# Moving a norm's logarithm, exponential and Newton step later in the first attention of a fused attention and feed-forward kernel

## The chip, the cores and the metric

The kernel runs on one core of a Trainium2 chip. The metric is the time of one execution on the device in microseconds (us); three runs of the kernel before the change were timed, and the median is what counts. One more execution was recorded by the hardware profiler.

## The reference

An attention with root-mean-square norms on queries and keys, followed by a feed-forward block with a squared ReLU, all in float32 (the feed-forward weights arrive as 64-bit floats):

```python
batch, n_heads, seq, head_dim = (8, 12, 448, 64)
def rmsnorm(x, g):
    rms = np.sqrt(np.mean(x * x, axis=-1, keepdims=True) + 1e-06)
    return x / rms * g
q_n, k_n = (rmsnorm(q, g_q), rmsnorm(k, g_k))
scores = np.matmul(q_n, k_n.transpose(0, 1, 3, 2)) / np.sqrt(64)
...  # softmax over the keys
attn_out = np.matmul(attn, v)
x = attn_out.transpose(0, 2, 1, 3).reshape(3584, 768)
h = x @ w_in                        # 768 x 2048
out = np.maximum(h, 0.0) ** 2 @ w_out   # 2048 x 768
```

## The kernel before, in words

The feed-forward block works on spans of two batch items (896 tokens); its two products use a seven-product block scheme, so that the weights are first turned into sums and differences of blocks. Heads are handled in pairs: 6 pairs per batch item, 12 pairs for a span. The kernel has these stages, one behind the other:

- a first pair's norm and transposes (`first_pair`);
- the first attention, `attention_alone`, for pairs 0 to 11 of span 0. Nothing but the preparation of the weights runs beside it. It ends at about 133 us, where the first product's matmuls (`pa`, L1091) begin;
- the first product of span 0, in which the rest of the weights is still prepared;
- then, span by span, products with the next span's attention (`attention`, another function) laid between them.

The order of the work is written out by hand: every engine issues its instructions in the order in which the Python code calls them, with semaphore waits put in where an operand needs them. Nothing is reordered by a scheduler. `attention_alone` is a generator with four `yield`s for each pair; at each `yield` the caller runs one or two quarters of a "tick" of the weights (`weights`, `prepare`). A tick rounds 128 rows or columns of a weight to float32. It has L589 and L606 on ScalarE, L603, L608 and L613 on VectorE, the block additions L575 and the sums L583 on GpSimd, loads (L540) and stores (L598) on SP's queue.

Iteration i of `attention_alone` does, between its yields:

1. the load of pair i+3 (L316 queries, L326 keys, on SP's queue); `scores(i, 0)` and `scores(i, 1)`, each of four matmul passes (L804) and two exponentials (L808); the transposes of pair i+1's keys (L779, copied out by L781); the `values` of pair i-1 with key chunks 2 and 3 (L867); `add_up(i, 1)`, a sum of two chunks of exponentials (L821); and `norm(i+2)`: squares on ScalarE (L719), their sums by head (L720), mean and epsilon (L721);
2. the transposes of pair i+1's queries (L779, scaled by L783); the load of values (L701); and `roots(i+2)`, the reciprocal square root of the norm: a logarithm (L730) and an exponential (L731) on ScalarE, one Newton step of three small VectorE instructions (L732 to L734), and on GpSimd the product of the raw queries with it (L735);
3. `scores(i, 2)` and `scores(i, 3)`; `total_of(i-1)`, the softmax sums by matmul (`tot`, L892); the `values` of pair i with chunks 0 and 1; and `finish(i-1)`: a transpose of the sums (L910), a reciprocal (L911), a transpose back (L912) and the product that gives the attention's output (L919), all on VectorE;
4. for odd pairs `add_up(i, 2)` (L821 again); `combine_x(i-1)` (L929 and L932 to L934 on VectorE) for the second batch item.

So `roots(i+2)` is called in iterations 1 to 9, for pairs 3 to 11. What it makes is used in two places: the normalised queries by the transposes L779 of iteration i+1, and the keys' factors as a scale of the exponentials L808 of iteration i+2. Logarithm and exponential share one buffer, `half`; the Newton step also uses `other`; both come from a pool with two buffers.

Of the kernel before, what the change touches and what calls it, by code (L numbers as in the profile page):

```python
# [304 lines left out]
def places_of(qk, i, work):  # L305


    first, second = i % 2 * 4 + work, i % 2 * 4 + 2 + (i // 2 + work) % 2
    return qk[:, first:second + 1:second - first]
# [78 lines left out]
def attention_then_ffn_bounded(  # L388
# [42 lines left out]
    SP = S // NJ  # L431
# [11 lines left out]
    NAT = 2 * NPAIR  # L443
# [21 lines left out]
    qk, qkT, ident, mhalf, gains, rstd0, _ = held  # L465
# [65 lines left out]
    spare, banks = {}, {}  # L531
# [142 lines left out]
    vs, probs, pavs, tots, normed, rstds = {}, {}, {}, {}, {}, {0: rstd0}  # L674
# [3 lines left out]
    def load(i):  # L678
        if i < NAT:
            load_q(nc, qk, q, i)  # L680
            load_k(nc, qk, k, i)
            return

        b, h0 = i // NPAIR, 2 * (i % NPAIR)
        for s, src in enumerate((q, k)):
            dst = by_squares(i, 0)[:, s]
            for n in range(4):
                nc.sync.dma_start(dst[n * 32:(n + 1) * 32],
                                  src[b, h0 + n // 2, :, n % 2 * 32:n % 2 * 32 + 32]
                                  .rearrange("(g t) e -> t g e", t=32))  # L690
# [32 lines left out]
    def roots(i):  # L723


        raw, sq = (places_of(qk, i, n)[:SP] for n in range(2))
        rstd = rstds[i]
        flat = rstd.rearrange("p s n -> p (s n)")
        y, t = (small.tile([P, 2 * S // 32], F32, tag=tag, name=tag)[:SP, 0:4 * NJ] for tag in ("half", "other"))
        nc.scalar.activation(y, flat, AF.Ln, scale=2.0 ** -63)  # L730
        nc.scalar.activation(y, y, AF.Exp, scale=-0.5, bias=sums["rebias"])  # L731
        nc.vector.scalar_tensor_tensor(t, y, -0.5, flat, ALU.mult, ALU.mult)  # L732
        nc.vector.tensor_tensor(t, t, y, ALU.mult)
        nc.vector.scalar_tensor_tensor(flat, t, 1.5, y, ALU.add, ALU.mult)  # L734
        nc.gpsimd.tensor_tensor(sq[:, 0].rearrange("p (j h d) -> p h j d", j=NJ, h=2),  # L735
                                raw[:, 0].rearrange("p (h j d) -> p h j d", j=NJ, h=2),
                                rstd[:, 0].rearrange("p (h j) -> p h j ()", h=2).to_broadcast([SP, 2, NJ, D]),
                                ALU.mult)
# [36 lines left out]
    def transpose(i, s, n):  # L775

        pt = bank("pt", n)
        for j in range(NJ):
            nc.tensor.transpose(pt[:, j * SP:(j + 1) * SP], normed[i][s][:, j * P:(j + 1) * P], ident[:SP, :SP])  # L779
        if s:  # L780
            nc.scalar.copy(qkT[:, i % 2, s], pt)  # L781
        else:
            nc.scalar.activation(qkT[:, i % 2, s], pt, AF.Copy, scale=gains[:, 0:1])  # L783

    def scores(i, c):


        if i >= NAT:
            sc = ps_s.tile([P, 2, 512], F32, tag="s", name="sc")
            n = S if c < NF else S // 2  # L790
            for h in range(2):
                rows = slice(h * D, (h + 1) * D)
                for m, part in enumerate(sides):
                    keys = slice(c * P + m * D, c * P + (m + 1) * D) if c < NF else slice(NF * P, S)
                    of = slice(0, S) if c < NF else slice(m * n, (m + 1) * n)
                    nc.tensor.matmul(sc[part, h, 0:n], qkT[rows, 0, 1, keys], qkT[rows, 0, 0, of], start=True, stop=True)  # L796
            pr = probs[i, c] = places[(NF * i + c) % len(places)] if c < NF else halves[i % 2]
            nc.scalar.activation(pr, sc[:, :, 0:n], AF.Exp)  # L798
            return
        at = i % 2  # L800
        sc = ps_s.tile([SP, 2, 512], F32, tag="s", name="sc")
        for h in range(2):
            rows = slice(h * D, (h + 1) * D)
            nc.tensor.matmul(sc[:, h, 0:S], qkT[rows, at, 1, c * SP:(c + 1) * SP], qkT[rows, at, 0, :],  # L804
                             start=True, stop=True)
        pr = probs[i, c] = places[(NJ * i + c) % len(places)][:SP]
        for h in range(2):
            nc.scalar.activation(pr[:, h], sc[:, h, 0:S], AF.Exp, scale=rstds[i][:, 1, 2 * c + h:2 * c + h + 1])  # L808

    def acc_of(i):  # L810
        return sums[i % 2][:SP] if i < NAT else sums["acc"]

    def add_up(i, c):

        acc = acc_of(i)
        if i >= NAT and c == NF:
            for m, rows in enumerate(sides):
                part = acc[rows, :, m * S // 2:(m + 1) * S // 2]
                nc.vector.tensor_tensor(part, part, probs[i, c][rows], ALU.add)
            return  # L820
        nc.vector.tensor_tensor(acc, probs[i, 0] if c == 1 else acc, probs[i, c], ALU.add)  # L821
# [59 lines left out]
    def added(i):  # L881

        return 3 if i % 2 and i + 1 < NAT else 2

    def total_of(i):


        tots[i] = ps_o.tile([P, S], F32, tag="t", name="tot")
        parts = [acc_of(i)] + [probs[i, c] for c in range(added(i), NJ)]
        for n, pr in enumerate(parts):  # L890
            for h in range(2):
                nc.tensor.matmul(tots[i][h * D:(h + 1) * D, :], sums["ones"], pr[:, h, :],  # L892
                                 start=(n == 0), stop=(n + 1 == len(parts)))
# [6 lines left out]
    def finish(i):  # L900

        b, hp = divmod(i, NPAIR)
        x = factors = xT[:, b % 2, hp]
        if i < NAT:
            pav = pavs.pop(i)


            turned, factors = sums["turned"], sums["factors"]
            few = small.tile([P, S // 32], F32, tag="few", name="few", bufs=1)
            nc.vector.transpose(turned, tots.pop(i))  # L910
            nc.vector.reciprocal(few, turned.rearrange("p (g r) -> p g r", r=32)[:, :, 0])  # L911
            nc.vector.transpose(factors.rearrange("p (g r) -> p g r", r=32),  # L912
                                few.rearrange("p g -> p g ()").to_broadcast([P, S // 32, 32]))

            x = x.rearrange("d (p j) -> d j p", j=NJ)
            pav, factors = (t.rearrange("d (j p) -> d j p", j=NJ) for t in (pav, factors))
        else:
            pav = rests.pop(i)
        nc.vector.tensor_tensor(x, pav, factors, ALU.mult)  # L919
        del vs[i]  # L920
# [15 lines left out]
    def attention_alone():  # L936


        for i in range(NAT):
            more = i + 1 < NAT  # L940
            if 0 < i < NAT - 3:
                load(i + 3)
            scores(i, 0)
            scores(i, 1)
            if i == 0:

                transpose(1, 1, 1)
                scores(0, 2)
                scores(0, 3)
                transpose(1, 0, 0)  # L950
                add_up(0, 1)
                norm(2)
                load_v(1)
                values(0, (0, 1))
                load(3)
                yield
                continue
            if more:
                transpose(i + 1, 1, 0)
            values(i - 1, (2, 3))  # L960
            add_up(i, 1)
            if i + 2 < NAT:
                norm(i + 2)
            elif not more:
                norm(NAT)
                load(NAT + 2)
            yield
            if more:
                transpose(i + 1, 0, 0)
            load_v(i + 1)  # L970
            if i + 2 < NAT:
                roots(i + 2)
            yield
            scores(i, 2)
            scores(i, 3)
            total_of(i - 1)
            values(i, (0, 1))
            finish(i - 1)
            yield
            if added(i) == 3:  # L980
                add_up(i, 2)
            combine_x(i - 1)
            if NAT <= i + 3 < NAT + 2:
                load(i + 3)
            yield
        values(i, (2, 3))
        total_of(i)
        finish(i)
        combine_x(i)
# [639 lines left out]
```

## Time and profile before

| what | us |
|---|---|
| runs | 1347.04, 1347.29, 1348.31; median 1347.29 |
| the profiled execution | 1347.79 |
| its span, first to last instruction | 1346.0 |
| TensorE busy in the span | 1324.7 (98%) |
| VectorE busy | 861.9 (64%) |
| ScalarE busy | 486.4 (36%) |
| GpSimd busy | 681.0 (51%) |
| first attention ends, L1091 begins | 133.1 |
| L730 and L731, 9 times each | 0.22 and 0.31 each |
| L732, L733, L734, 9 times each | 0.17 each |
| L735, 9 times | 1.04 to 1.54 each, median 1.14 |

In the profile PE is TensorE, PEld its weight load, DVE VectorE, ACT ScalarE, POOL GpSimd, SP the queue of SyncE. A line such as L821 is a line of the kernel's file. An instruction is written as what it writes, an arrow to the left, and what it reads, with partitions and elements. The shares of busy time are averages over all stages; the change lies in the first tenth of the span, so that what counts is the view of that stretch. The granted TensorE clock is full speed (0.999 on the mean).

### The profile page before, as it was taken

To read this page: it belongs to the slowest core of one execution; us is meant where nothing else is said; L and a number is where in the kernel's file an instruction comes from. 1 tells how busy PE (TensorE), PEld (TensorE's weight loads), DVE (VectorE), ACT (ScalarE), POOL (GpSimd) and SP (SyncE) were. 2 spreads that over 40 slices of the span, in tenths; PEclk is the share of its full clock that TensorE was granted. 3 is DMA by queue.
4 is the path that set the end of the run, shared out by engine and by line. 5 is a ranking of instruction groups with operands and counts; after the bars stand their busy time and mean duration, and the time that the engine had idled before them with its cause. 6 is when DMAs were issued, how large, how long until landed. Compare 5 with 4: busy or idle time off the path is not lost.

```text
span 1346.0 us, 17761 instructions
## 1 busy us (share of the span) xinstructions
PE 1324.7 (98%) x5930; PEld 698.9 (52%) x5930; DVE 861.9 (64%) x1333; ACT 486.4 (36%) x939; POOL 681.0 (51%) x546
## 2 busy tenths in 40 slices
PE   8999999999999999999999999999999999999997
PEld 3333444444445655444444755444444665556887
DVE  6999788489988233467888533457888823336553
ACT  7886466555541011345553011235554101111000
POOL 5766533466765222647774522447676522322452
PEclk9999999999999999999999999999999999999999
DMA  8977999666665433346755433345664444421333
GB/s 226 244 214 200 312 357 331 187 131 121 138 140 125 104 88 88 102 105 132 149 125 144 110 90 88 92 113 117 134 129 128 107 100 139 131 88 47 115 103 56
DMA packets 413817, 190.18 MB, mean 141 GB/s; under 512 B 282388, under 2 KB 408724, under 8 KB 413716
## 3 DMA queue, kind: packets, MB, share of 16 engines
q1 hardware_dynamic: 406164, 180.21, 51.8%
q0 software_dynamic: 4736, 8.40, 2.5%
q8 instruction: 49, 0.80, 0.3%
q10 hardware_dynamic: 2816, 0.34, 0.2%
q14 instruction: 52, 0.43, 0.1%
HBM read 155.72 MB, written 33.16 MB: 140 GB/s over the span
## 4 chain that ended last, share of the span: by engine, by line
PE 87%; DVE 7%; ACT 4%; issue 1%; DMA 1%; POOL 0%; SPq 0%; DVEq 0%; ACTq 0%
PE ps L1190 21%; PE pd L1091 11%; PE pa L1091 10%; PE pc L1091 10%; PE sc L796 7%; PE pav L878 7%; PE pb L1091 5%; PE ps L1373 3%; PE ps L1241 2%; PE pd L1345 2%; PE pc L1345 2%; PE pa L1345 2%; ACT gT L808 2%; PE pd L1175 1%; PE pc L1175 1%
## 5 line engine op out<-in xcount | busy, mean ns | idle before, releaser
L1067 POOL TENSOR_TENSOR gT<-gT 128x448 f32<-128x448 f32 x96 | 94.2, 983 | 258.0 <-ACT gT L1063 258.0
L761 POOL TENSOR_TENSOR half<-half,mhalf 128x28 f32<-128x28 f32 x36 | 184.1, 5115 | 70.2 <-DVE half L760 56.2
L1190 PE MATMUL ps<-gT,sw 128*128 128x448 f32 x432 | 169.3, 545 | 0.0
L1063 ACT ACTIVATE gT<-gT 128x448 f32<-128x448 f32 x96 | 55.4, 577 | 300.5 <-DVE gT L1106 300.5
L1091 PE MATMUL pa<-xT,sw 128*128 128x448 f32 x384 | 155.0, 540 | 0.6 <-ACT p L1095 0.6
L1190 PEld LDWEIGHTS ps<-gT,sw 128*128 128x128 f32 x432 | 80.1, 190 | 87.2 <-issue 85.2
L1190 PE MATMUL ps<-gC,sw 128*128 128x448 f32 x288 | 113.1, 546 | 0.0
L796 PE MATMUL sc<-qkT 64*64 64x448 f32 (+1 forms) x1152 | 110.1, 497 | 0.3 <-ACT pr L798 0.2
L1091 PEld LDWEIGHTS pa<-xT,sw 128*128 128x128 f32 x384 | 72.7, 190 | 71.8 <-issue 70.5
L583 POOL TENSOR_TENSOR gC<-gC 128x384 f32<-128x384 f32 x64 | 76.4, 1213 | 63.4 <-DVE gC L579 61.7
L1190 PEld LDWEIGHTS ps<-gC,sw 128*128 128x128 f32 x288 | 53.2, 190 | 59.5 <-issue 57.7
L846 POOL DMA_DIRECT2D xT<-factors x72 | 38.1, 534 | 89.9 <-DMA factors<-square 65.2
L1106 DVE TENSOR_TENSOR gT<-z,pd 128x448 f32<-128x448 f32 x32 | 19.8, 620 | 97.8 <-PE pd L1091 97.8
L798 ACT ACTIVATE pr<-sc 128x896 f32<-128x896 f32 x87 | 76.9, 909 | 11.1 <-PE sc L796 11.1
L1091 PE MATMUL pd<-xT,sw 128*128 128x448 f32 x192 | 77.9, 542 | 1.5 <-DVE z L1098 1.4
L763 POOL TENSOR_TENSOR qk<-qk,half 128x448 f32<-128x448 f32 x72 | 76.9, 1089 | 2.8
L1091 PE MATMUL pd<-xC,sw 128*128 128x448 f32 x192 | 77.5, 540 | 0.7 <-DVE gT L1106 0.7
L1091 PE MATMUL pb<-xC,sw 128*128 128x448 f32 x192 | 77.5, 540 | 0.2 <-DVE gT L1106 0.2
L1091 PE MATMUL pc<-xT,sw 128*128 128x448 f32 x192 | 77.5, 540 | 0.0
L1091 PE MATMUL pc<-xC,sw 128*128 128x448 f32 x192 | 77.4, 539 | 0.0
L878 PE MATMUL rest<-pr,vt 64*64 64x448 f32 x348 | 72.7, 537 | 0.0
L878 PE MATMUL pav<-pr,vt 64*64 64x448 f32 x348 | 72.7, 537 | 0.0
(282 smaller groups left out, 2455.1 us busy)
## 6 DMA issues: line engine op xcount, KB each, us to landing
sw<-w1s SPq DMA_DIRECT2D x224, 192.0 KB, 2.4
sw<-w2s SPq DMA_DIRECT2D x102, 256.0 KB, 3.5
w1s<-gC SPq DMA_DIRECT2D x8, 1344.0 KB, 6.9
w2s<-gC SPq DMA_DIRECT2D x8, 1344.0 KB, 6.8
qk<-in_q_dram SPq DMA_DIRECT2D x144, 56.0 KB, 2.6
qk<-in_k_dram SPq DMA_DIRECT2D x144, 56.0 KB, 2.4
xT<-factors POOLq DMA_DIRECT2D x72, 112.0 KB, 3.4
vt<-in_v_dram SPq DMA_DIRECT2D x72, 96.0 KB, 3.8
```

Of the source, the lines that this page charges most:

```text
L583: nc.gpsimd.tensor_tensor(*[blocks_of(n)[:, place_of(n, i)] for i in (dst, x, y)], op)
L761: nc.gpsimd.tensor_tensor(half, half, mhalf, ALU.pow)
L763: nc.gpsimd.tensor_tensor(qkn[:, s], raw[:, s], half[:, s * NG:(s + 1) * NG].rearrange("p g -> p g ()").to_broadcast([P, NG, 32]), ALU.mult)
L796: nc.tensor.matmul(sc[part, h, 0:n], qkT[rows, 0, 1, keys], qkT[rows, 0, 0, of], start=True, stop=True)
L798: nc.scalar.activation(pr, sc[:, :, 0:n], AF.Exp)
L878: nc.tensor.matmul(into, vs[i][rows, h, c, :], probs[i, c][rows, h, :], start=(c == 0), stop=(c == NF), skip_group_check=True)
L1063: nc.scalar.activation(g, src, AF.Relu)
L1067: nc.gpsimd.tensor_tensor(g, g, g, ALU.mult)
L1091: nc.tensor.matmul(ps, stream[n + at][:, c], rhs[:, c], start=first and c == 0, stop=c == HC - 1, skip_group_check=not first)
L1190: nc.tensor.matmul(ps, stream[n][:, c % 4], rhs_of[i][:, c], start=c == 0, stop=c == HF - 1)
L1345: nc.tensor.matmul(ps, lhs[:, c], rhs[:, c], start=first and c == 0, stop=c == HK - 1, skip_group_check=not first)
L1373: nc.tensor.matmul(ps, weights_of(o, m, c // HK)[:, c % HK], rhs_of[i][:, c, part], start=c == 0, stop=c == HF - 1)
```

## The change

`roots` is cut in two. Its logarithm and exponential stay in `roots`, which is called behind `scores(i, 3)` instead of ahead of the yield before it. The Newton step and the product on GpSimd become a function `step`, called behind `finish(i-1)`. The buffers are handed over in a dictionary, `spare`. No instruction is added, removed or altered. The quarters of a weights tick that run at the yield between come ahead of the moved instructions.

```diff
         nc.scalar.activation(y, flat, AF.Ln, scale=2.0 ** -63)
         nc.scalar.activation(y, y, AF.Exp, scale=-0.5, bias=sums["rebias"])
+        spare["root", i] = y, t
+
+    def step(i):
+
+        raw, sq = (places_of(qk, i, n)[:SP] for n in range(2))
+        rstd = rstds[i]
+        flat = rstd.rearrange("p s n -> p (s n)")
+        y, t = spare.pop(("root", i))
         nc.vector.scalar_tensor_tensor(t, y, -0.5, flat, ALU.mult, ALU.mult)
         nc.vector.tensor_tensor(t, t, y, ALU.mult)
         nc.vector.scalar_tensor_tensor(flat, t, 1.5, y, ALU.add, ALU.mult)
...
             load_v(i + 1)
-            if i + 2 < NAT:
-                roots(i + 2)
             yield
             scores(i, 2)
             scores(i, 3)
+            if i + 2 < NAT:
+                roots(i + 2)
             total_of(i - 1)
             values(i, (0, 1))
             finish(i - 1)
+            if i + 2 < NAT:
+                step(i + 2)
             yield
```

On ScalarE L730 and L731 stand behind the four exponentials L808 of scores 2 and 3, and behind the tick's L589 or L606 of that yield. On VectorE L732 to L734 stand behind L919. On GpSimd L735 stands behind the weights' instructions of that yield: it is moved past none to four of L575 and L583.

## The prediction

> **What bounds it.** Over the whole page TensorE is busy 98% of the span, but the change acts only in the first attention, from about 23 us to 114 us, so I read that stretch by itself. The view of stages gives, per 30 us, busy time of PE, PEld, DVE, ACT and POOL:
>
> ```profile
> 30.00:60.00 30.00, 28.07 (x146) 10.94 (x148) 28.36 (x43) 25.59 (x47) 19.11 (x15) 1.00 0.99 241
> 60.00:90.00 30.00, 28.17 (x146) 10.39 (x142) 28.00 (x41) 23.96 (x44) 21.10 (x18) 1.00 0.86 260
> 90.00:120.00 30.00, 28.33 (x148) 10.87 (x148) 29.01 (x40) 24.02 (x43) 21.74 (x16) 1.00 0.64 176
> ```
>
> VectorE (third figure) and TensorE (first) are both at 93 to 97%; ScalarE has 4 to 6 us of slack in each 30. Next, the waits from 20 to 133 us: waiter, what it waited for, us in total, times, longest.
>
> ```profile
> ACT half L730 <- DVE rstd L721: 14.7, 9, 2.6
> ...
> POOL qk L735 <- DVE rstd L734: 12.4, 4, 3.7
> ...
> PE pt L779 <- ACT qkT L781: 3.4, 7, 1.1
> ...
> DVE other L732 <- ACT half L731: 1.4, 6, 0.6
> ...
> DVE gT L821 <- ACT gT L808: 0.9, 1, 0.9
> ```
>
> Almost all of ScalarE's idle time stands before the logarithm L730. VectorE itself waits for another engine only 1.4 + 0.9 us, and 0.2 for a square. So VectorE sets the pace, and how long its own instructions take is the question. From the groups by shape in 24.86 to 117 us (count, busy us, mean ns):
>
> ```profile
> L821 DVE TENSOR_TENSOR gT<-gT 112x896 f32<-112x896 f32 x14 | 22.2, 1595 | 0.9 <-ACT gT L808 0.9
> L608 DVE TENSOR_SCALAR gC<-gC 128x768 uint32<-128x768 uint32 x11 | 11.2, 1014 | 0.1
> ...
> L603 DVE TENSOR_SCALAR gC<-gC 128x768 f32<-128x768 f32 x11 | 7.3, 666 | 0.1
> ```
>
> These means are not the true durations. The timeline has L821 at 1.08 us where GpSimd is idle and at 1.9 us where it is at work; L608 and L603 at 0.55 or 0.9 to 2.8; L613 at 0.95 or 1.3 to 1.7. I call such a lengthened instruction a hit. Between 24.86 and 117 us I count 22, and the excess is 22.2 - 14x1.08 = 7.1 for L821, 11.2 - 11x0.55 = 5.1 for L608, 1.3 for L603, 1.9 for L613, 0.5 for L721: 15.9 us, or 0.72 us a hit. The transposes and products of `finish` (L910 to L919, 2.45 us) and the reduction L720 (1.2 us) are never hit.
>
> **The skill.** The Trainium skill, "SBUF — State Buffer", section "Who interferes with whom", says that a VectorE instruction in a two-port mode, or with two SBUF inputs against a GpSimd instruction that reads SBUF, and GpSimd lock each other out of a shared port pair, whoever is second waiting for the whole instruction; reductions and instructions with one SBUF input outside those modes don't. The trace agrees: 0.82 us more on the two-input L821, none on L720 or L910. "ScalarE: Activation LUTs", section "Table sets: the hidden batching unit", has Ln and Exp in one set; the trace has a single table load, at 0.73 us, so I cost putting Ln between other Exps at nothing.
>
> **The parts.** Nothing is added or removed; 9 norms (pairs 3 to 11) are moved. Call "turn i" the stretch from the Newton step of iteration i to that of i+1.
>
> Ln and Exp (0.22 + 0.31 us, 9 times) go behind the four exponentials L808 of scores 2 and 3. ScalarE's 14.7 us disappear and L808 comes earlier. ScalarE isn't the bound, so this is worth only what others waited for it: the 1.4 us before L732, the 0.9 before L821 and 0.2 before L720, together **-2.5 us** at most. What is late next on ScalarE is L783, which needs the transposed queries.
>
> The Newton step (three instructions, 0.62 us with their gaps) goes behind `finish`. It then finds its exponential long done. But L735, the product on GpSimd that it releases, now starts about 3 us later against VectorE's work. Two rows of the timeline (start us, length us) show the old place, over `finish`, 0.2 us behind the end of Newton at 55.42 (the releaser named, L589, had long ended):
>
> ```profile
> 55.34 0.64 DVE L910 STREAM_TRANSPOSE gT<-tot 128x448 f32<-128x448 f32 x1
> 55.65 1.04 POOL L735 TENSOR_TENSOR qk<-qk,rstd 112x512 f32<-112x512 f32 x1 [2.05 <-ACT gC L589]
> ```
>
> GpSimd's weight work (L575, L583, about 1.0 us each unhit, four or so a turn) queues behind L735 in order. Before, L735 and one or two of those ran under `finish`. After, GpSimd stands waiting for Newton during `finish`, and L735 with its followers runs against L603, L608, L613 and L821. Some weight work is now ahead of L735 and gets the 1.2 us of L720, but that holds one instruction, `finish` two and a half.
>
> I walked the new order of issue for turns 1 to 8: the first VectorE instruction behind Newton goes free (L735 starts 0.2 us after L734), then the engines take the lock in turn, and the instruction right behind an L821 goes free, as in the trace at 71.28. Turn 4 as example. Before: Newton, `finish` (over it L735, L575, L583), L603, L608, L821, L720, L721, L613: the trace has three hits (58.37, 60.50, 63.55). After: Newton, L603 free, L735, L608 hit, L583, L821 hit, L583 and the start of L575 under L720, L613 hit, L575, L603 hit, `finish`: four. By turns, before as seen 1, 3, 3, 3, 3, 1, 3, 2 = 19; after by the walk 3, 4, 3, 4, 3, 4, 5, 2 = 28 (in turn 2 one of the four falls on Newton itself). The same walk over the old order gives 23, so it counts high; the added hits lie between 28 - 23 = 5 and 28 - 19 = 9. I take 7: 7 x 0.72 = **+5.0 us**.
>
> L735 also has a reader, the query transposes L779 of the next iteration. Before, L735 ended 4.0 to 4.7 us ahead of them (46.26 against 50.31). Newton moves by 2.5 to 4.7 us and L735 waits for one VectorE instruction more, so that margin goes; TensorE queues the scores 2 and 3, the totals L892 and the values L867 behind that transpose. While VectorE is behind, that wait is cover, not cost: the loop L910 to L919 2.45, Newton 0.62, wait and L735 1.8, transposes 0.75, scores 1.69, totals 1.65 or 2.48 is about 9.4 us against a turn of 10.4 (83.07 us for 8). At the end of the stage it isn't cover. L779 of pair 11 starts at 113.74, and from there TensorE runs nearly unbroken to 133 us. Newton of iteration 9 follows `finish` at 111.3; add L821 and L929, which go first (1.6), L735 (1.04) and its signals (0.3): 114.2. That is **+0.45 us** besides VectorE's own slip.
>
> Moved past queues: SP's load of a later pair's queries (L316) waits for L735 and delays the keys, values and weight words behind it by some 3 us; but a load issued at 56.72 is squared by L719 at 70.92, so 14 us cover it. If that cover went, L719 would wait. GpSimd issues no DMA here. L575 and L583 ahead of L735 finish some blocks of weights sooner, whose store (L598) waited 21.2 us in all for L583; no engine waited for that store in this stage: nothing.
>
> Sum: -2.5 + 5.0 + 0.45 = **+3.0 us** (2.95), carried to the end, since everything up to 191 us is issued in one fixed order with the weights. The profiled execution took 1347.79 us (span 1346.0 and 1.8 around it), so it would take 1350.8; the runs' median, 1347.29, stands 0.5 below it, so I say 1350.3.
>
> **Unseen, bounded.** The trace shows no turn with L735 behind `finish`. From below: no hit added, only the waits gone, -2.5 + 0.45 = -2.0; the hits may even fall, as VectorE had one of 2.27 us (L608 at 79.45) that needn't recur: -4. From above: 9 hits at a full GpSimd instruction of 1.0 us, +7.0.
>
> **Rivals.** 0.2%, or 2.7 us, is about what a measurement of this kernel can tell from no change.
>
> One, *lock-out decides* (the above): +1.5 with 5 hits, +4.4 with 9; likeliest +3.0; own range 1347.5 to 1352. For it: 19 hits already, and `finish` as the only long shelter. Against: the walk overcounts.
>
> Two, *ScalarE's release decides*, faster: the chain of waits runs through L808 often (12.3% of it in 86 to 120 us), so a freed ScalarE may bring TensorE and VectorE forward. It decides if fewer than 3 hits are added (3 x 0.72 = 2.05), and passes 0.2% if the hits fall by one or more: about -3.2 us, 1344.1.
>
> Three, *TensorE waits for L735*: if L779 is held 0.5 us in each of 8 turns with nothing to cover it, 4 us come on top: +7, 1354.3. Against: the loop of 9.4 us.
>
> Four, *absorbed*: from 163 to 191 us the chain leaves TensorE for the weights' rounding (L589, L603, L608, L579). If the weights' DMA (busy share 1.00 in 150 to 180 us) and not the engines' order sets that, a slip before it vanishes: within 1 us, 1347.3. That the change doesn't do what it says is excluded: the issue orders show the moves in all 9 iterations.
>
> **Chances.** One 0.50, two 0.22, three 0.13, four 0.15. One falls within 0.2% about one time in ten (0.05), four always: same 0.20; slower 0.45 + 0.13 = 0.58; faster 0.22. The range takes in two and three: 1344.0 to 1355.0; beyond either end lies about 0.1.
>
> **What would show it.** Right: L730's wait on L721 gone; L735 starting after L919; hits in 24 to 117 us near 29, L821's mean above 1.7 us; L779 waiting for L735; 'pa' L1091 starting near 136 instead of 133.1. Wrong: mean durations of L821, L608, L613 unchanged or lower, and the first L1091 earlier than 133; or a later start there and the same end, which would be the fourth case.

## The result, and the profile after

The kernel became slower. Median before 1347.28 us (6 runs, 1345.68 to 1348.31), after 1353.55 us (6 runs, 1351.88 to 1355.8): ratio 1.0047, 95% interval 1.0037 to 1.0056. The forecast was 1350.3 us with a range of 1344 to 1355, so the direction is right and the size is 3.3 us short. It lies above the 1347.5 to 1352 us that the prediction gave to the lock-out alone. The profiled execution of after took 1353.08 us, its span 1351.3 us, 5.3 above that of before.

Lines of the changed file carry other numbers: L721 and everything above it keep theirs, L730 and L731 too; L732 to L734 are now L740 to L742; then, before to after, L735 is L743 (the product on GpSimd), L779 L787 (transposes), L783 L791, L804 L812 (scores), L808 L816, L821 L829 (`add_up`), L867 L875, L892 L900 (totals), L910 to L912 L918 to L920, L919 L927, L929 L937, L1091 L1101 (`pa`).

First the view by stages: length, busy time of PE, PEld, DVE, ACT, POOL, then granted clock, DMA share, GB/s.

```profile
30.00:60.00 30.00, 27.32 (x142) 10.79 (x144) 29.23 (x42) 25.46 (x46) 22.16 (x16) 1.00 0.85 236
60.00:90.00 30.00, 28.12 (x148) 10.78 (x144) 29.06 (x40) 24.44 (x45) 22.58 (x15) 1.00 0.75 227
90.00:120.00 30.00, 25.49 (x128) 10.01 (x124) 27.22 (x37) 21.26 (x38) 20.89 (x14) 0.94 0.77 196
```

VectorE is busier than before in the first two stages (29.23 and 29.06 against 28.36 and 28.00) and does fewer instructions there (42 and 40 against 43 and 41). Its instructions got longer. In the third stage something else happens: both TensorE and VectorE fall, and the clock is 0.94.

The groups by shape, VectorE in 24.86 to 121 us (count, busy us, mean ns, idle before):

```profile
L829 DVE TENSOR_TENSOR gT<-gT 112x896 f32<-112x896 f32 x14 | 25.0, 1794 | 0.0
L608 DVE TENSOR_SCALAR gC<-gC 128x768 uint32<-128x768 uint32 x11 | 9.7, 878 | 0.2
...
L603 DVE TENSOR_SCALAR gC<-gC 128x768 f32<-128x768 f32 x10 | 5.5, 550 | 0.0
L721 DVE TENSOR_SCALAR rstd<-rstd 112x16 f32<-112x16 f32 x8 | 5.5, 686 | 0.3
```

The mean of `add_up` goes from 1595 to 1794 ns, 12 of its 14 instructions now being hit. L603 is hit no more (666 to 550), L608 less often (1014 to 878), but the tiny L721, 241 ns on the mean before, now takes 686. Its work is 0.17 us; I read the rest as waiting for the port lock, which the trace shows as busy time.

Then the waits in 20 to 133 us (waiter, what it waited for, us in all, times, longest):

```profile
PEld pt L787 <- POOL qk L743: 14.3, 8, 4.6
...
ACT gT L816 <- PE sc L812: 11.4, 10, 1.7
...
PE pt L787 <- POOL qk L743: 8.2, 5, 3.8
ACT qkT L791 <- PE pt L787: 6.7, 5, 3.3
...
DVE gT L918 <- PE tot L900: 3.3, 3, 2.2
...
ACT half L730 <- DVE rstd L721: 1.9, 2, 1.2
```

ScalarE's wait before the logarithm fell from 14.7 to 1.9 us, and VectorE's waits for ScalarE (1.4 and 0.9) are gone. But the time that ScalarE had stood before the logarithm it now stands before exponentials and query copies, since TensorE is late: TensorE itself waits 8.2 us for the product on GpSimd, a wait that before had no row. And VectorE waits for TensorE's totals.

Last the timeline of TensorE, where that wait is longest (start, length, in brackets the idle time ahead and its releaser):

```profile
105.79 0.92 PE L787 MATMUL pt<-ident,qk 112*128 112x112 f32 x4 [3.84 <-POOL qk L743]
106.64 3.08 PE L812 MATMUL sc<-qkT 64*112 64x448 f32 x8
109.65 2.48 PE L900 MATMUL tot<-gT,ones 112*64 112x448 f32 x12
```

And VectorE's answer to it:

```profile
112.17 0.65 DVE L918 STREAM_TRANSPOSE gT<-tot 128x448 f32<-128x448 f32 x1 [2.15 <-PE tot L900]
```

The four transposes take 0.92 us and the eight scores passes 3.08 behind this gap; elsewhere in this trace, at 118.17 us, they take 0.60 and 1.76. The granted clock of 105 to 110 us is 0.66. The Trainium skill, "TensorE: Matmul & The Clock Gate", section "What's actually happening", has this mechanism: an idle window of some 3.4 us halves the clock. Here a gap of 3.84 us was followed by about 4 us at roughly half speed.

**The balance.** From the Newton step of iteration 1 to that of iteration 9 before took 83.07 us, after 87.54: +4.47. It consists of the waits for ScalarE, -2.5; of the hits, 26 with an excess of 18.4 us against 19 with 13.9, +4.5; and of VectorE's waits for the totals in turns 1 to 8, +2.4 (2.15 of it in the row above). The Newton step stands at another point of VectorE's order than before, so I carry on from an instruction that both kernels have at the same one: the `add_up` behind `finish` of iteration 9 starts at 111.27 us before and 115.14 after, 3.87 later, 0.6 less than the turns say. The end of the stage adds 0.56 to that, and from the last query transposes to `pa` come another 0.85. So `pa` begins at 138.42 instead of 133.14 us, 5.28 later, and the span is 5.3 longer. Nothing was given back.

### The profile page after: what moved, and what is told of

Read it like the earlier page. It is cut to its first block, busy times and chain, and to the rows that moved or that the text cites. A ratio compares the mean times of both kernels' runs of the same rounds, so it can differ in the third digit from the quotient of the medians.

```text
span 1351.3 us, 17755 instructions
## 1 busy us (share of the span) xinstructions
PE 1324.9 (98%) x5930; PEld 700.2 (52%) x5930; DVE 868.2 (64%) x1333; ACT 486.9 (36%) x939; POOL 688.4 (51%) x546
## 4 chain that ended last, share of the span: by engine, by line
PE 90%; DVE 5%; ACT 2%; issue 1%; POOL 1%; DMA 1%; SPq 0%; DVEq 0%; ACTq 0%; POOLq 0%
PE ps L1200 21%; PE pd L1101 11%; PE pa L1101 10%; PE pc L1101 10%; PE sc L804 7%; PE pav L886 7%; PE pb L1101 5%; PE ps L1383 3%; PE sc L812 2%; PE ps L1251 2%; PE pd L1355 2%; PE pa L1355 2%; PE pc L1355 2%; PE tot L900 1%; PE pav L875 1%; PE pd L1185 1%
## 5 line engine op out<-in xcount | busy, mean ns | idle before, releaser
L1101 PE MATMUL pa<-xT,sw 128*128 128x448 f32 x384 | 155.0, 540 | 0.7 <-ACT p L1105 0.7
L804 PE MATMUL sc<-qkT 64*64 64x448 f32 (+1 forms) x1152 | 110.0, 496 | 0.3 <-ACT pr L806 0.2
L1101 PEld LDWEIGHTS pa<-xT,sw 128*128 128x128 f32 x384 | 72.7, 190 | 71.9 <-issue 70.6
L583 POOL TENSOR_TENSOR gC<-gC 128x384 f32<-128x384 f32 x64 | 72.9, 1158 | 63.4 <-DVE gC L579 61.6
L1101 PE MATMUL pd<-xT,sw 128*128 128x448 f32 x192 | 77.9, 542 | 1.5 <-DVE z L1108 1.3
L1101 PE MATMUL pd<-xC,sw 128*128 128x448 f32 x192 | 77.5, 540 | 0.7 <-DVE gT L1116 0.7
L1101 PE MATMUL pb<-xC,sw 128*128 128x448 f32 x192 | 77.5, 540 | 0.1
L1101 PE MATMUL pc<-xC,sw 128*128 128x448 f32 x192 | 77.4, 539 | 0.0
L1101 PE MATMUL pc<-xT,sw 128*128 128x448 f32 x192 | 77.4, 539 | 0.0
```

Of the source, the lines that this page charges most:

```text
L583: nc.gpsimd.tensor_tensor(*[blocks_of(n)[:, place_of(n, i)] for i in (dst, x, y)], op)
L1101: nc.tensor.matmul(ps, stream[n + at][:, c], rhs[:, c], start=first and c == 0, stop=c == HC - 1, skip_group_check=not first)
```

## The experiments

Ratios are to the kernel before, with 95% intervals. "Turns" is the time from the Newton step of iteration 1 to that of 9 in the profiled execution; hits are counted in the same stretch. The numbers, gathered:

| kernel | median us | ratio | turns | hits, excess us | `pa` begins |
|---|---|---|---|---|---|
| before | 1347.28 | 1 | 83.07 | 19, 13.9 | 133.14 |
| after | 1353.55 | 1.0047 (1.0037 to 1.0056) | 87.54 | 26, 18.4 | 138.42 |
| e1_release | 1348.35 | 1.0011 (1.0004 to 1.0018) | 83.76 | 23, 16.6 | 134.0 |
| e2_step | 1355.75 | 1.0071 (1.0049 to 1.0092) | 90.21 | 22, 15.7 | 141.28 |
| e4_norm_first | 1345.28 | 0.9979 (0.9969 to 0.9989) | 79.80 | 16, 11.4 | 131.12 |
| e6_product | 1347.67 | 1.0001 (0.9992 to 1.001) | 83.52 | 23, 15.0 | 134.04 |
| e9_on_vector | 1349.25 | 1.002 (1.0013 to 1.0027) | 87.97 | 20, 13.4 | 136.30 |
| e11_late_transposes | 1351.02 | 1.0031 (1.0019 to 1.0043) | 86.56 | 26, 18.4 | 137.26 |
| e12_first_and_late | 1346.44 | 0.9997 (0.9989 to 1.0005) | 81.39 | 14, 9.9 | 131.92 |

### The two halves of the change, each alone

Both moved steps behind the scores, but the Newton step ahead of the totals and `finish` (e1_release, against after):

```diff
             scores(i, 3)
             if i + 2 < NAT:
                 roots(i + 2)
+                step(i + 2)
             total_of(i - 1)
             values(i, (0, 1))
             finish(i - 1)
-            if i + 2 < NAT:
-                step(i + 2)
```

> The logarithm and exponential where the change puts them, behind the exponentials of scores 2 and 3, but the Newton step and its GpSimd product ahead of finish, so that the product again runs over finish. Theory A (the port lock decides: the place of the GpSimd product against finish): lengthened VectorE instructions in the first attention near 19 to 23 as before, not 26, ScalarE's 14.7 us before L730 gone, and a time at or below before: 1344.8 to 1347.5 us. Rival B (the later logarithm and exponential are what costs): the Newton step now waits on VectorE for an exponential that stands behind four others, 1 us or more in each of 9 iterations, and the time stays above before by 3 to 7 us.

Only the Newton step behind `finish`, logarithm and exponential in their old place (e2_step, against after):

```diff
             load_v(i + 1)
+            if i + 2 < NAT:
+                roots(i + 2)
             yield
             scores(i, 2)
             scores(i, 3)
-            if i + 2 < NAT:
-                roots(i + 2)
             total_of(i - 1)
```

> Only the Newton step and its GpSimd product move behind finish; logarithm and exponential stay where they were. Theory A (port lock, product late): about 26 lengthened VectorE instructions as in the changed kernel, while ScalarE keeps its wait for L721; so as slow as the change or up to 2.5 us slower: 1352 to 1357 us. Rival B (the later logarithm and exponential are what costs): near before, 1346.5 to 1348.5 us.

Measured against before: logarithm late alone +1.3 us (1348.35 against 1347.01), Newton step late alone +8.7 (1355.75 against 1347.01), both +6.3. So the loss is the Newton step's, and it is there without the other half. With the Newton step late, the late logarithm gives back some 2.4 us (the intervals of e2 and after overlap by a little); on its own it gains nothing. e1 came out between its two expectations, 0.85 us above the one and below the other: ScalarE's wait before L730 was to be gone and was still 10.1 us, and 4 hits came on top. In e2 VectorE waited 3.2 us for exponentials and 3.3 for totals, and the clock of 90 to 120 us was 0.89. Its hits, 22, are fewer than after's, yet it is the slowest: hits are not the whole of it. Why the logarithm's place changes the hits at all was not settled; it shifts every engine's phase a little.

### Is it GpSimd's order, or the time at which the product is released?

The Newton step as before, and only the call of the product behind `finish`, so that it stands behind the weights' work on GpSimd as in after (e6_product, against before):

```diff
-        nc.gpsimd.tensor_tensor(sq[:, 0].rearrange("p (j h d) -> p h j d", j=NJ, h=2),
...
+    def product(i):
...
+        nc.gpsimd.tensor_tensor(sq[:, 0].rearrange("p (j h d) -> p h j d", j=NJ, h=2),
...
             finish(i - 1)
+            if i + 2 < NAT:
+                product(i + 2)
```

> The kernel before, with only the call of the GpSimd product moved behind finish; logarithm, exponential and Newton step stay. The GpSimd queue then has the changed kernel's order, but the product is released as early as before. Theory A (what costs is that the product is released only behind finish): near before, lengthened VectorE instructions 19 to 24, 1346 to 1348.5 us. Rival D (what costs is the order on GpSimd's queue, weight work ahead of the product): 1350 to 1354 us.

1347.67 against 1347.33 us in the same batch: no difference that the interval shows. So the order on GpSimd's queue by itself isn't what costs; what is left is the late Newton step, which releases the operand late. The hits did rise to 23 with an excess of 15.0 us, 1.1 us over before, and the turns by 0.45.

### Taking the product off GpSimd

If the lock is what makes the change dear, the product must cost less on VectorE, although VectorE sets the pace (e9_on_vector, against after; L743 is then the product on VectorE):

```diff
-        nc.gpsimd.tensor_tensor(sq[:, 0].rearrange("p (j h d) -> p h j d", j=NJ, h=2),
+        nc.vector.tensor_tensor(sq[:, 0].rearrange("p (j h d) -> p h j d", j=NJ, h=2),
```

> The changed kernel with the product of the raw queries on VectorE instead of GpSimd, right behind the Newton step, as the first three pairs already have it (0.69 us there). No release of GpSimd behind finish any more and no wait of TensorE for it. Theory A (port lock): 9 products add 9 x 0.6 to 0.7 = 5.4 to 6.3 us to VectorE and take about 9 of its waits of 0.72 us away, and GpSimd's weight work runs over finish again: 1347 to 1351 us. If the lock played no part, VectorE's added work comes on top: 1357 to 1360 us; less what TensorE's waits cost (up to 3.7 us), 1354 us or more.

Groups by shape, VectorE, 24.5 to 118 us:

```profile
L829 DVE TENSOR_TENSOR gT<-gT 112x896 f32<-112x896 f32 x13 | 18.1, 1397 | 0.0
L743 DVE TENSOR_TENSOR qk<-qk,rstd 112x512 f32<-112x512 f32 x9 | 8.5, 940 | 0.3
```

VectorE got nine products more, 0.69 us each where unhit, and the kernel came down from 1.0047 to 1.002, disjoint intervals, about 3.6 us. The mean of `add_up` fell from 1794 to 1397 ns. On the instructions that after has as well, hits fell from 26 to 17 and their excess from 18.4 to 11.2 us; three of the products were hit themselves, which makes 20 and 13.4. In the eight turns this is a draw: 5.0 us less of hits against eight products, 5.5 us, and the turns take 87.97 us instead of 87.54. TensorE's wait before the transposes stayed what it was (6.8 for the product and 1.3 put down to L608, 8.1 in all), with a gap of 3.76 us at 106.28 us and slow scores behind it.

The gain in the profiled execution comes behind the turns. The `add_up` behind `finish` of iteration 9 starts 1.2 us later than in after, the last query transposes 0.3 earlier, and `pa` 2.1 earlier: from those transposes to `pa` it takes 18.41 us instead of 20.25. In that stretch five of VectorE's instructions are lengthened in after (3.4 us in all) and none in e9, and ScalarE's wait for L757 is 1.7 us instead of 3.6. Where the rest of the 3.6 lies was not followed. So the added work was paid for with hits that went, and TensorE's lateness hardly changed: this shows the lock as a real cost of the change, but not that it is the larger one in the turns.

### Less work on GpSimd: a pair that didn't tell

The sums L583 left out in the ticks of the first attention, without and with the change (e7_few_before, e8_few_after):

```diff
-            if there(n) and n % 2:
+            if there(n) and n % 2 and n >= EARLY // 4:
...
+        nc.vector.memset(stage[:, 0:BLOCKS * 8 * HW], 0.0)
```

> The kernel before, without the sums of weight blocks (L583) in the first attention's ticks, over blocks zeroed once at the start by VectorE; GpSimd keeps the product and the two L575 of each tick, about 3 us of work a turn instead of 5. To be read only against the changed kernel with the same left out. Theory A (port lock): nearly all of GpSimd's work fits over finish, lengthened VectorE instructions fall from 22 to 8 or fewer, L821's mean from 1.60 to below 1.3 us.

> The changed kernel with the same left out (no L583 in the first attention's ticks, blocks zeroed once). Theory A (port lock): 1 to 2 lengthened VectorE instructions a turn are left, VectorE at 9.1 to 9.8 us a turn about level with TensorE's 9.6, and the distance to the same kernel without the change shrinks from 6.3 to 1 to 3.5 us. Rival B2 (the late product itself, for which TensorE waits, costs the time): the distance stays at 5 to 7 us.

1347.2 us (ratio 1.0, 0.9991 to 1.0009) and 1354.32 us (1.0049, 1.0032 to 1.0066): the distance is 7.1 us, not shrunk to 1 to 3.5; the number is nearer to what the rival, lateness alone, had expected. A row of each, groups by shape in 26 to 121 us, first without the change:

```profile
L821 DVE TENSOR_TENSOR gT<-gT 112x896 f32<-112x896 f32 x15 | 17.9, 1198 | 2.6 <-ACT gT L808 2.5
```

and with it:

```profile
L829 DVE TENSOR_TENSOR gT<-gT 112x896 f32<-112x896 f32 x14 | 24.2, 1737 | 1.1 <-ACT gT L816 1.1
```

The working of the expectation was wrong. With so few operations, GpSimd fits nearly all of them over `finish` in the old order (5 hits in turns 1 to 8), while behind a late Newton step the product and the block additions that remain still meet VectorE (19 hits). The change adds more hits here, not fewer, so that lock and lateness grow together (turns 76.97 against 83.66 us), and the pair tells nothing between them. Against before, e7 shows one thing more: with some 10.7 us fewer of hits its turns are 6.1 us shorter, which fits VectorE setting the pace. The total doesn't show it, because zeroing the blocks holds VectorE for 5.18 us at 10.10 us, and the work behind the Newton step of iteration 1 starts 6.6 us later than before; `pa` begins at 133.5 us.

### The slow clock after TensorE's wait

Does the half-speed stretch at 105 us cost time? Filler matmuls ahead of the last query transposes but one were to keep TensorE busy. The first try stood one iteration too early (e3_warm, against after):

```diff
+        for _ in range(8 if i == 9 and not s else 0):
+            nc.tensor.matmul(pt, ident, qkT[:, (i - 1) % 2, 0, :], start=True, stop=True)
```

> The changed kernel with 8 matmuls of 448 columns (16 passes[...]) that are overwritten at once, issued ahead of the query transposes of pair 9, where TensorE stood idle for 3.84 us and then ran scores at 3.08 instead of 1.76 us. Theory C (the idle stretch lowers TensorE's clock, and VectorE's 2.15 us wait for the totals follows from it): the stretch of slow matmuls and that wait vanish, and the time falls 1.5 to 2.2 us below the changed kernel, to 1351 to 1352.2 us. Rival (the late start alone makes VectorE wait, the clock doesn't matter): within 0.5 us of the changed kernel or above it.

The gap stands ahead of pair 10's transposes, and in `transpose` `i` is the pair, so the filler filled no gap. It held the transposes of pair 9 until 98.92 us instead of 92.62; with TensorE that much later, the gap of 3.84 us and its slow stretch didn't occur in this execution, and the time was no better: 1354.38 us, ratio 1.0061 (1.0044 to 1.0078). With `i == 10`, 8 fillers (e5_warm10) and 4 (e10_warm_short):

> The changed kernel with the 8 overwritten matmuls ahead of the query transposes of pair 10, the iteration in which TensorE stood idle for 3.84 us and came back slow (in the run before they stood one iteration too early). Theory C (the lowered clock costs VectorE's 2.15 us wait for the totals): granted clock 1.00 throughout, the scores behind it at 1.76 us, the first matmul of the first product 1 to 2 us earlier than the changed kernel's 138.42 us, 1351 to 1352.5 us. Rival (the clock's loss is covered): within 0.5 us of the changed kernel.

> As the run with 8 overwritten matmuls ahead of pair 10's query transposes, but with 4 (8 passes; 16 took 6.28 us, 0.39 each, and held the transposes to 108.1 us, so these take 3.1 us and end before the product does). Theory C: transposes near 105.8 us as in the changed kernel, scores at 1.76 us, VectorE's wait for the totals down from 2.15 to 0.7 us or less, first matmul of the first product at 136.7 to 137.5 instead of 138.42 us, 1351.5 to 1352.5 us. Rival: within 0.5 us of the changed kernel.

Eight were too many: each call makes two passes of 0.39 us, 6.28 us in all, which held the transposes until 108.12 us. The scores ran at full speed (1.76 us), but VectorE now waited 2.65 us: 1353.61 us, ratio 1.0052 (1.0034 to 1.0069). Four came out at 1352.46, ratio 1.0041 (1.0026 to 1.0057), which overlaps after's interval, so the times don't settle it. `pa` came no earlier in either (139.08 and 139.72 us), against both expectations. In the trace of the four the stretch itself is shorter; VectorE's timeline (this file's lines stand two further down: transposes L789, scores L814, totals L902):

```profile
113.48 0.65 DVE L920 STREAM_TRANSPOSE gT<-tot 128x448 f32<-128x448 f32 x1 [0.52 <-PE tot L902]
```

The wait is 0.52 us instead of 2.15, and from the totals of iteration 8 to those of 9 it takes 13.18 us instead of 14.81: 1.63 less. But this execution came to the stage 1.25 us later and had another stretch of slow clock at 84 us, behind a gap of 1.89 us. In after the gap at that place is 1.85 us and the clock stays up: there VectorE waits 0.24 us for the totals, in e10 1.88, and turn 6 takes 10.2 us against 11.8, with the same three hits. So the traces show twice that a slow stretch costs some 1.6 us, and the slow clock as the cause of most of that one wait. Its share of the median was not measured: the six runs of after have mean granted clocks of 0.994 to 0.997, the two slowest (1354.27 and 1355.8 us) the lowest and the fastest (1351.88) the highest, so the number of such stretches may differ from run to run.

### TensorE's wait for the product itself

The query transposes called behind the scores 2 and 3 instead of ahead of them, so that a late product is asked for later (e11_late_transposes, against after):

```diff
-            if more:
-                transpose(i + 1, 0, 0)
...
             scores(i, 3)
+            if more:
+                transpose(i + 1, 0, 0)
```

> The changed kernel with the query transposes of the next pair (and their copy on ScalarE) behind scores 2 and 3 instead of ahead of them, which gives the product 1.7 us more before TensorE needs it. Theory A with lateness as its smaller part: TensorE's waits for the product (8.2 us) mostly gone, VectorE's for the totals (3.3 us) below 1, lengthened VectorE instructions still about 26; 1349.5 to 1352 us. Rival B2 (lateness is nearly all of it): 1346 to 1348.5 us.

1351.02 us, ratio 1.0031: about 2.2 us (0.0016) come back of the 6.3, though the intervals overlap; `pa` comes 1.2 us earlier in the trace. The hits stay as they are, 26 with 18.4 us. TensorE's waits for the product were to be mostly gone and VectorE's for the totals below 1 us; they are 5.2 and 1.6. One gap and its slow clock remain, with the totals in place of the scores behind it (timeline, PE):

```profile
105.50 1.01 PE L787 MATMUL pt<-ident,qk 112*128 112x112 f32 x4 [3.56 <-POOL qk L743]
106.44 4.69 PE L900 MATMUL tot<-gT,ones 112*64 112x448 f32 x12
```

So e11 took away only a part of the lateness, and neither e9 nor e11 measures the lock or the lateness alone. That the lock is the larger part rests on the balance of the trace, 4.5 us of hits against 2.4 of waits for the totals.

### Norm ahead of `add_up`: a version that is faster

If the wait before the logarithm is to go, the norm can come earlier instead of the logarithm later. In the kernel before, `norm(i + 2)` is called ahead of `add_up(i, 1)` (e4_norm_first):

```diff
-            add_up(i, 1)
             if i + 2 < NAT:
                 norm(i + 2)
+            add_up(i, 1)
```

> The kernel before with one thing altered: in each iteration from 1 the next norm's sums (L720, L721) are issued on VectorE ahead of add_up(i, 1) (L821) instead of behind it, so that the logarithm is released 1 to 1.9 us sooner and nothing else moves on ScalarE or GpSimd. If ScalarE's release is worth what VectorE waited for it: 1345 to 1347 us, ScalarE's wait before L730 down from 14.7 to below 4 us. If a sooner Newton step brings the GpSimd product into L608 and L613 instead of finish: more lengthened instructions than 22 and 1348 to 1351 us.

1345.28 us, ratio 0.9979 (0.9969 to 0.9989): better than both kernels. `pa` begins at 131.12 us, 2.0 earlier than before. ScalarE's wait before the logarithm was expected below 4 us and is 9.3. Its rows, waits in 20 to 133 us:

```profile
ACT half L730 <- DVE rstd L721: 9.3, 9, 2.0
...
DVE rstd L720 <- DMA qk<-in_k_dram: 1.3, 1, 1.3
DVE rstd L720 <- ACT qk L719: 1.2, 3, 0.6
```

and groups by shape, VectorE in 24.5 to 117 us:

```profile
L821 DVE TENSOR_TENSOR gT<-gT 112x896 f32<-112x896 f32 x14 | 19.2, 1369 | 0.0
```

VectorE's waits for the exponential L731 and for `add_up`'s operand are gone, as in after, and the Newton step stays ahead of `finish`, so the product stays under it: 16 hits instead of 19, and `add_up`'s mean is 1369 ns instead of 1595. VectorE pays 2.3 us of waits at L720 in the stretch of that row. How much of the gain is the waits and how much the hits was not separated.

Both ideas together, the norm first and the query transposes late (e12_first_and_late), against before:

> The kernel before with the norm's sums ahead of add_up(i, 1), as in the run that gave 1345.3 us, and the next pair's query transposes behind scores 2 and 3. There TensorE still waited 2.2 us for ScalarE's copy of the keys' transposes ahead of them. If these waits lie on the path: 1343 to 1345 us. If they are cover for VectorE: 1344.8 to 1346 us, no gain over that run.

1346.44 us, ratio 0.9997 (0.9989 to 1.0005), outside both expectations. The hits stay low (14), but in the waits L720 stands 5.2 us for its squares L719 and TensorE's scores L804 5.7 us for the copies L783 of the late transposes. With the product early, moving its reader late only makes the next scores late. e4_norm_first alone stays the best version.

## Why the prediction was right, and where it fell short

- **VectorE sets the pace, so its lengthened instructions decide.** Right. The excess of hits grew by 4.5 us (5.0 predicted), at 0.71 us a hit (0.72 predicted). By turns the walk gave 3, 4, 3, 4, 3, 4, 5, 2; the trace has 3, 4, 3, 3, 3, 3, 5, 2, that is 26: the 7 added hits that were taken between the walk's 5 and 9. In 24.86 to 121 us, where the same work now ends, there are 28; "near 29" was announced. Where they fall was only partly right: turn 4 was told as L608, `add_up`, L613, L603, and is L608, `add_up`, L721:

```profile
60.50 1.28 DVE L608 TENSOR_SCALAR gC<-gC 128x768 uint32<-128x768 uint32 x1
61.70 1.88 DVE L829 TENSOR_TENSOR gT<-gT 112x896 f32<-112x896 f32 x1
63.51 1.21 DVE L720 TENSOR_REDUCE rstd<-qk 112x16 f32<-112x1024 f32 x1
64.75 0.71 DVE L721 TENSOR_SCALAR rstd<-rstd 112x16 f32<-112x16 f32 x1
```

Beside them GpSimd, with the product no longer under `finish` (which ended at 59.55 us):

```profile
60.23 1.14 POOL L743 TENSOR_TENSOR qk<-qk,rstd 112x512 f32<-112x512 f32 x1 [1.28 <-DVE rstd L742]
61.33 3.12 POOL L583 TENSOR_TENSOR gC<-gC 128x384 f32<-128x384 f32 x2
64.42 3.25 POOL L575 TENSOR_TENSOR gC<-words,gC 128x384 int32<-128x384 int32 x2
```

- The reduction L720 runs unhit at 1.21 us while GpSimd goes ahead, and the instruction behind it pays. The walk had used L720 as shelter and then charged L613.
- **The gain of 2.5 us from VectorE's waits.** Right in after: all three are gone. e1 shows the limit of it: the same release without a late Newton step gained nothing. The 2.5 was worked out as "at most", and the sum used all of it.
- **Edits costed at nothing.** The logarithm between exponentials, the later loads and stores: no wait of an engine that they caused appears in the stage. SP's queue waits 38.4 us for the product instead of 20.2, and that stays covered; the one wait of an engine for a load, 1.1 us of L589 at 27.23, ends ahead of the first moved product (27.91). The order on GpSimd's queue by itself shows no cost either (e6).
- **TensorE's wait for the product.** This step failed, by its size. The prediction said "While VectorE is behind, that wait is cover, not cost", from a loop of 9.4 us against a turn of 10.4, an average. But the turns are uneven: turn 7 has five hits, VectorE is then late with the Newton step of iteration 8 and what follows, and TensorE stood 3.84 us. It came back at a low clock, which stretched transposes and scores by 0.32 + 1.32 us, and the totals came 2.15 us too late for VectorE. The term should have been +2.4 and stood at 0. The third rival had the mechanism, with +4 at 0.5 us a turn; in fact nearly all of the cost came from one large wait. e11, which asks for the product later, got 1.2 us back in the trace.
- **The end of the stage.** +0.45 predicted; the last query transposes came 0.56 late besides VectorE. But "TensorE runs nearly unbroken to 133 us" didn't hold: from there to `pa` it took 20.25 us instead of 19.40, +0.85. In it the last values wait 1.14 us for an exponential where it was 0.30 before, and ScalarE waits 3.62 us instead of 2.75 for VectorE's L757 (L749 before).
- **Carried to the end.** Right: +5.28 at `pa`, +5.3 in the span. The fourth rival, a slip absorbed by the weights' DMA, is wrong here. The second, a gain from ScalarE, is wrong for this change, but half its idea is what e4 uses.
- The sum of the steps, 2.95, thus lacks 2.4 for TensorE's wait and the slow clock and 0.96 for the end, and has 0.5 too much of hits; less the 0.6 by which the turns overstate the slip of VectorE that is 5.2, against 5.3 measured in the profiled execution.
- Luck had a part in the range. The first case alone was given 1347.5 to 1352; 1353.55 is inside the whole range because that also took in the third rival, which had a chance of 0.13 and 1354.3 us. What happened is the first case with a part of the third.
- One sum of the second rival is off: 3 x 0.72 is 2.16. The 2.05 there is 2.5 - 0.45, what the hits have to outweigh. Nothing else rests on it.

## What to carry to other kernels

An operand that is released later doesn't only wait: the work that it releases on another engine moves to another place, and if the two engines lock each other out of memory, the question is which instructions it will then run beside. Put it beside those that are not hit, here under `finish`, and remove the wait from the other side, by making its input earlier (e4) rather than its reader later. And a margin taken as an average over turns doesn't cover the longest turn, whose gap can bring a slow clock with it.

## What the runs showed of the hardware

- A tiny instruction pays the lock as well: L721 on 112x16 values went from 0.17 us to between 0.69 and 0.83 in seven of eight turns, because the reduction ahead of it lets GpSimd go on. The Trainium skill, "SBUF — State Buffer", section "Who interferes with whom", lets reductions pass, and the trace agrees with L720 at 1.21 us each time.
- The clock fell at gaps shorter than the 3.4 us cited above from the Trainium skill's "TensorE: Matmul & The Clock Gate". A gap of 1.89 us in e10 (timeline, PE) was enough:

```profile
83.90 0.99 PE L789 MATMUL pt<-ident,qk 112*128 112x112 f32 x4 [1.89 <-POOL qk L743]
84.82 3.01 PE L814 MATMUL sc<-qkT 64*112 64x448 f32 x8
```

- In after, a gap of 1.85 us at about the same place was not:

```profile
82.61 0.60 PE L787 MATMUL pt<-ident,qk 112*128 112x112 f32 x4 [1.85 <-POOL qk L743]
83.14 1.76 PE L812 MATMUL sc<-qkT 64*112 64x448 f32 x8
```

- So gap length alone doesn't decide; what does was not tried.
